# Pairing the heads in the features as they are paired in the work: new loads of a weight matrix, new sums, a new order

## The chip, the core and the metric

The kernel runs on one core of a Trainium2 chip. A core has TensorE (matrix products, written to PSUM), VectorE (DVE), ScalarE (ACT), GpSimd (POOL), SyncE (SP, which here only issues transfers), an on-chip memory (SBUF) of 128 partitions, and 16 DMA engines that carry the transfers between device memory and SBUF. The metric is the device time of one execution in microseconds, as the median of several runs.

## The reference

Causal attention over 4 batches, 8 heads, 768 positions of 64 features. Heads 0, 2 and 6 see everything up to their own position ("retrieval"); heads 1, 3, 4, 5 and 7 see the first 4 positions and a window of the last 64. Then a feed-forward layer over all 3072 tokens, with the 8 x 64 attention outputs as the 512 features:

```
scores = q @ k.T / sqrt(64)
a = softmax(where(mask[head], scores, -1e9))
x = (a @ v) laid out as (3072 tokens, 8 heads x 64)
h = x @ w_in                          # 512 x 2048
g = h * sigmoid(beta * h)
out = g @ w_out                       # 2048 x 512, float32
```

All inputs and the output are float32; the kernel computes its products in bfloat16.

## The kernel before

The work is cut into 8 units of 384 query positions, two for each batch: u = 0 is the first half of a sequence, u = 1 the second; a unit's number is n = 2b + u. For each unit the kernel transposes queries and keys, computes scores, exponentials and masks, sums and products with V (`attention`), normalizes them into `xT` (features in partitions, tokens in columns), and runs the feed-forward layer: 16 blocks of hidden features through `mm1`, tanh and multiply (`first`), and 48 matmuls of `mm2` into three output tiles (`second`).

The 512 features stand in `xT` as four tiles of 128 partitions, two heads each. `PAIRS` (line 17) says which two heads share a tile of queries and keys, `XT` (line 18) which two share a tile of features. In the kernel before these differ in the first two tiles: `PAIRS` has (0, 2), (1, 3), while `XT` has (1, 0), (2, 3). `mm1` multiplies tile t of `xT` with tile t of `w_in`, so the rows of `w_in` must stand in the order of `XT`.

`load_w_in(s)` (line 473), for s = 0 to 3, brings a quarter of `w_in`'s columns (512 rows of 2 KB, 1 MB) into a staging tile `wf` of 128 partitions x 4 row tiles: one transfer for tiles 1 to 3, and one of 64 partitions for each half of tile 0, because its two heads stand in swapped order. `load_w_out(s)` brings 1 MB of `w_out` in one transfer. `wf` has three buffers, which later loads of q, k and v use too. POOL casts each quarter in four pieces into `w_in_sb`; four blocks of `mm1` need one quarter.

For units 2 to 7, the softmax sums go this way: `sums_d` (line 748) has TensorE add up each head's row in a PSUM bank, with the heads placed by `QUARTERS` and `ROWS`; `sums_copy` brings them to SBUF (`sc`); `sums_turn` (line 781) moves the rows into `rec`, 12 partitions a head, with one small transfer for each entry of `TURNS` (line 31), which are (first row, step, slot, number of rows); VectorE takes reciprocals; `spread_rows` moves `rec` into four rows of `R`, and `spread_lanes` copies these over the partitions. `norm` multiplies. Units 0 and 1 have another path for this, on TensorE.

All transfers but four at the start are issued by SP, in one queue. The order of the whole program is written out: `_Plan.add` collects 1102 operations with the engines that may do them, a cost and what they need; `SEQUENCE` (line 37) lists them in an order found beforehand, and `CHOICE` (line 92) names the engine of each of the 97 operations that have a choice. `_Plan.run` goes through the list, works out start times from the costs, hands out buffers, and gives the operations out by start time. On each engine they keep the order of `SEQUENCE`. In unit 0 and in `sink_rows`, `fill` puts extra matmuls on TensorE where the plan leaves it a gap.

Each engine works its list in order; a transfer on SP waits for its buffer, and for the semaphore of an earlier transfer, before it is issued, and everything behind it in the queue waits too.

Of the kernel before, what the change touches and what calls it, by code (L numbers as in the profile page):

```python
# [16 lines left out]
PAIRS = [(0, 2), (1, 3), (4, 5), (6, 7)]  # L17
XT = [(1, 0), (2, 3), (4, 5), (6, 7)]
# [10 lines left out]
QUARTERS = [[[1, 0], [4, 5], [2, 3], [6, 7]], [[2], [6], [0], [5, 1, 4, 3, 7]]]  # L29
ROWS = [16, 1]  # L30
TURNS = [[(0, 32, 0, 4), (16, 32, 4, 4)], [(97, 1, 0, 2), (0, 32, 2, 4), (99, 1, 6, 2)]]
# [6 lines left out]
    0, 472, 8, 10, 480, 2, 12, 14, 77, 485, 484, 474, 477, 1, 479, 4, 6, 9, 475, 481, 25, 33, 11, 35, 3, 27,  # L38
    13, 34, 483, 36, 53, 26, 42, 37, 15, 28, 44, 54, 78, 5, 39, 40, 38, 7, 100, 45, 55, 469, 29, 30, 47, 56,
    79, 80, 101, 89, 90, 57, 43, 31, 32, 41, 85, 470, 48, 471, 102, 112, 103, 50, 59, 51, 91, 60, 92, 114, 86,  # L40
    108, 116, 58, 81, 82, 49, 104, 115, 113, 134, 117, 109, 16, 135, 17, 23, 137, 138, 61, 52, 46, 62, 118,
    139, 105, 87, 88, 119, 110, 83, 84, 106, 120, 24, 140, 122, 121, 136, 123, 18, 19, 20, 63, 107, 21, 22,
    73, 74, 64, 75, 141, 111, 65, 66, 71, 67, 125, 159, 160, 76, 68, 69, 70, 126, 486, 487, 490, 128, 129,
    131, 132, 142, 143, 488, 72, 526, 530, 489, 534, 538, 124, 127, 130, 133, 496, 497, 500, 527, 528, 531,
    532, 535, 536, 539, 542, 543, 540, 498, 544, 546, 547, 548, 499, 553, 554, 555, 506, 507, 557, 558, 559,
    561, 562, 563, 510, 161, 162, 184, 508, 509, 95, 96, 565, 566, 567, 569, 93, 97, 94, 98, 99, 516, 518,
    144, 145, 185, 576, 577, 146, 570, 517, 571, 155, 157, 578, 156, 158, 519, 147, 148, 149, 580, 581, 150,
    151, 520, 193, 167, 196, 511, 515, 512, 514, 501, 513, 153, 152, 154, 503, 584, 505, 585, 588, 582, 194,
    598, 502, 586, 476, 599, 600, 589, 590, 602, 606, 610, 614, 607, 608, 603, 604, 611, 612, 615, 616, 491,
    492, 618, 619, 620, 625, 629, 168, 626, 627, 504, 494, 633, 171, 630, 637, 641, 634, 631, 635, 638, 639,  # L50
    648, 652, 169, 493, 529, 642, 495, 643, 649, 650, 653, 654, 170, 188, 189, 533, 172, 592, 593, 173, 174,
    190, 191, 521, 656, 657, 163, 523, 164, 524, 594, 537, 165, 166, 186, 522, 525, 658, 187, 192, 541, 545,
    549, 550, 552, 219, 220, 221, 556, 560, 203, 206, 207, 564, 204, 660, 664, 665, 666, 661, 222, 568, 572,
    575, 223, 226, 198, 201, 199, 601, 605, 609, 482, 573, 662, 613, 617, 225, 621, 624, 628, 224, 205, 175,
    176, 200, 195, 197, 202, 208, 209, 178, 177, 179, 229, 228, 227, 236, 632, 237, 238, 240, 239, 230, 233,
    579, 583, 587, 241, 243, 232, 242, 180, 591, 636, 478, 250, 244, 640, 644, 647, 210, 211, 251, 252, 231,
    271, 273, 253, 645, 245, 248, 246, 247, 595, 551, 596, 574, 254, 651, 249, 181, 212, 255, 655, 256, 659,
    663, 182, 258, 183, 213, 215, 622, 217, 257, 275, 259, 260, 261, 214, 667, 216, 218, 670, 646, 668, 671,
    674, 678, 672, 272, 682, 686, 675, 676, 679, 680, 683, 318, 288, 684, 687, 688, 690, 276, 279, 691, 692,
    697, 698, 699, 701, 705, 702, 274, 703, 278, 709, 706, 707, 262, 263, 710, 713, 720, 711, 724, 281, 721,  # L60
    722, 277, 320, 280, 292, 234, 714, 715, 725, 726, 291, 293, 728, 729, 730, 732, 736, 322, 319, 323, 264,
    295, 737, 733, 623, 669, 673, 321, 235, 677, 297, 300, 324, 734, 298, 681, 685, 689, 738, 693, 694, 302,
    305, 303, 289, 301, 325, 696, 700, 265, 266, 267, 306, 282, 283, 285, 268, 269, 270, 704, 708, 712, 716,
    717, 299, 327, 296, 294, 304, 742, 746, 290, 750, 326, 743, 744, 747, 748, 328, 337, 335, 370, 751, 752,
    307, 718, 338, 754, 339, 284, 755, 758, 759, 308, 340, 342, 756, 341, 760, 286, 762, 769, 773, 777, 336,
    763, 764, 349, 374, 373, 377, 774, 775, 309, 778, 350, 779, 329, 770, 771, 310, 311, 372, 719, 723, 380,
    781, 782, 785, 727, 783, 371, 352, 375, 786, 787, 792, 695, 343, 287, 793, 794, 344, 345, 347, 348, 796,
    800, 801, 802, 378, 797, 798, 376, 379, 731, 354, 357, 346, 358, 312, 313, 804, 805, 808, 355, 356, 735,
    739, 740, 314, 316, 315, 317, 390, 745, 806, 749, 753, 809, 810, 353, 391, 392, 394, 417, 395, 351, 418,
    757, 814, 815, 761, 765, 766, 767, 816, 330, 818, 819, 822, 826, 830, 820, 823, 824, 827, 828, 396, 397,  # L70
    387, 831, 832, 359, 360, 768, 834, 841, 835, 842, 836, 421, 843, 332, 331, 772, 333, 399, 361, 334, 362,
    776, 780, 784, 788, 791, 845, 846, 401, 847, 849, 789, 795, 422, 404, 850, 405, 851, 597, 393, 853, 854,
    857, 398, 799, 420, 424, 855, 858, 859, 402, 864, 865, 868, 869, 803, 866, 872, 876, 403, 870, 400, 880,
    873, 874, 363, 381, 364, 365, 807, 811, 812, 790, 406, 368, 407, 881, 882, 419, 423, 366, 367, 817, 813,
    821, 877, 825, 829, 878, 833, 837, 838, 369, 886, 887, 890, 894, 382, 408, 409, 384, 888, 891, 892, 895,
    896, 840, 898, 899, 902, 906, 900, 903, 904, 383, 907, 908, 427, 425, 426, 436, 435, 437, 438, 913, 917,
    410, 411, 921, 922, 923, 918, 919, 844, 385, 848, 852, 386, 914, 915, 388, 389, 428, 431, 925, 926, 927,
    439, 441, 440, 856, 860, 412, 861, 863, 415, 413, 414, 929, 936, 416, 930, 937, 938, 931, 867, 871, 940,
    839, 941, 942, 434, 448, 451, 452, 875, 879, 883, 449, 884, 443, 444, 445, 958, 962, 446, 447, 963, 964,
    959, 960, 944, 948, 949, 450, 950, 453, 945, 946, 966, 970, 741, 974, 967, 968, 971, 972, 975, 976, 889,  # L80
    430, 885, 978, 952, 953, 954, 979, 893, 980, 897, 901, 905, 909, 912, 454, 456, 457, 455, 442, 985, 986,
    987, 458, 916, 459, 460, 910, 989, 990, 993, 997, 429, 432, 433, 991, 862, 998, 999, 461, 462, 920, 924,
    928, 932, 935, 939, 933, 1001, 1008, 994, 995, 1012, 1013, 1014, 1009, 943, 947, 951, 955, 1010, 1002,
    1003, 1016, 473, 1020, 1021, 956, 463, 464, 961, 465, 466, 467, 1024, 1025, 1022, 965, 969, 973, 934, 468,
    1030, 1017, 1018, 977, 1026, 981, 982, 984, 1031, 1032, 983, 1034, 1038, 1035, 1036, 988, 992, 1039, 1042,
    1040, 1043, 1046, 1044, 1047, 1048, 1050, 1051, 1052, 996, 1057, 1061, 1065, 1058, 1059, 911, 1062, 1063,
    1066, 1067, 1000, 1004, 1005, 1007, 1069, 1070, 1073, 1071, 1074, 1075, 1079, 1080, 1081, 957, 1011, 1082,
    1085, 1083, 1084, 1015, 1086, 1087, 1088, 1091, 1089, 1092, 1033, 1037, 1041, 1045, 1090, 1049, 1006,
    1093, 1053, 1056, 1054, 1060, 1064, 1068, 1072, 1076, 1055, 1077, 1019, 1023, 1027, 1028, 1078, 1094,
    1095, 1029, 1098, 1096, 1097, 1099, 1100, 1101,  # L90
]
CHOICE = (
    "dgddadggggdddaaddaadgggaadadgdggdgggddddaadadaadgadaddagdadgdddgagggdggaaaaaadaaaaadaaaadadadadda"
# [95 lines left out]
def kernel(  # L189
# [15 lines left out]
    B, H, S, D = q.shape  # L205
# [267 lines left out]
    def load_w_in(s):  # L473
        f = stg.tile([128, 2048], F32, name="wf", bufs=RINGS["wf"]).rearrange("p (a n) -> p a n", a=NP)

        def rows(r, n, tiles):
            return bass.AP(moe_w_in.tensor, moe_w_in.offset + r * d_ff + s * 2 * FS,
                           [[d_ff, n], [128 * d_ff, tiles], [1, 2 * FS]])
        sp.dma_start(out=f[:, 1:4, :], in_=rows(128, 128, 3))
        sp.dma_start(out=f[0:D, 0:1, :], in_=rows(D, D, 1))  # L480
        sp.dma_start(out=f[D:128, 0:1, :], in_=rows(0, D, 1))
        wst["i", s] = f
# [706 lines left out]
    for u in range(2):  # L1189
        add("dve", 0.75, lambda u=u: const_mask_new(u), gives=[("const", "new", u)],  # L1190
            needs=[("M", u, pi, ri) for pi in range(NP) for ri in range(len(rounds_of(pi, u))) if mask_cost(pi, ri, u)] + [("const", "mask", 0)])
        add("dve", [0.9, 0.7][u], lambda u=u: const_mask_s(u), needs=[("const", "m")], gives=[("const", "mask", u)])
# [56 lines left out]
```

## Time and profile before

| | |
|---|---|
| time, median of 3 runs | 246.41 us (244.87 to 246.75) |
| the profiled execution | 243.74 us, of which 242.0 from its first to its last instruction |
| busy: TensorE, VectorE, ScalarE, POOL | 221.8, 161.5, 138.9, 87.8 us |
| mean granted TensorE clock | 0.993 |
| read from device memory, written | 27.57 MB, 6.29 MB |
| `mm1`, 512 matmuls of 128x384 | 91.5 us busy |
| `mm2`, 375 matmuls of up to 128x512 that the trace holds | 87.4 us busy |

Busy times come from the records of one execution; products on TensorE are pipelined, so their busy time is a bound on the time that it has work. Each line of a chain or a timeline begins with its start and its duration in microseconds. Almost every instruction carries line 112 (a helper through which all are issued), so the names of the tiles tell them apart: `b<-xT,w_in` is `mm1`, `b<-w_out,gT` is `mm2`, `wf<-in_moe_w_in_dram` a load of `w_in`, `rec<-sc` the turn of the sums, `R<-rec` their spreading. A letter q behind an engine (SPq) means its queue of instructions that issue transfers or wait.

### The profile page before, as it was taken

Reading aid. Unit: us, or ns where it says so; the run is one execution under the profiler, and the core shown is the slowest. Engines: PE = TensorE matmul, PEld = TensorE weight load, DVE = VectorE, ACT = ScalarE, POOL = GpSimd, SP = SyncE. Lnnn points to the kernel's source line nnn. Section 1 sums busy time; section 2 is a strip of 40 time slices with the busy share of each in tenths; the row PEclk is TensorE's granted clock in tenths of the full one; section 3 lists DMA queues with packets and bytes.
Section 4 is the critical chain, followed back from the end, with each engine's and each line's share of the span. In section 5 each row is a group of like instructions: output and inputs, shape, how many; then the busy total and the mean of one; then the engine's idle time right before and its main releaser. Section 6 shows DMA issues by size and latency. Waiting matters only on the chain.

```text
span 242.0 us, 6040 instructions
## 1 busy us (share of the span) xinstructions
PE 221.8 (92%) x2327; PEld 125.8 (52%) x2352; DVE 161.5 (67%) x390; ACT 138.9 (57%) x232; POOL 87.8 (36%) x200
## 2 busy tenths in 40 slices
PE   7788888899999888797999899999999999999995
PEld 7545454465544454453555455555555555655544
DVE  5879957887383658777679458877777465655311
ACT  2878854784537647553895675517668543346300
POOL 6441673687605247313751725350390000000000
PEclk9979999999999999999999999999999999999999
DMA  6999999999999396889979971746901011031022
GB/s 203 309 235 286 252 216 315 352 325 214 202 191 221 72 255 121 154 222 170 253 156 179 152 168 48 173 118 74 217 3 43 3 47 47 3 130 44 2 87 88
DMA packets 90003, 38.41 MB, mean 159 GB/s; under 512 B 76518, under 2 KB 82934, under 8 KB 89974
## 3 DMA queue, kind: packets, MB, share of 16 engines
q1 hardware_dynamic: 88886, 37.24, 66.4%
q10 hardware_dynamic: 1088, 0.79, 1.0%
q8 instruction: 18, 0.29, 0.5%
q14 instruction: 11, 0.09, 0.1%
HBM read 27.57 MB, written 6.29 MB: 140 GB/s over the span
## 4 chain that ended last, share of the span: by engine, by line
PE 54%; DMA 21%; SPq 13%; POOL 4%; DVE 4%; issue 3%; ACT 1%; POOLq 0%; DVEq 0%
PE b L112 49%; SPq L112 13%; DMA wf<-in_moe_w_in_dram 10%; PE sp L112 4%; DMA QK<-c 4%; DMA wf<-in_k_dram 3%; DMA q2f<-in_q_dram 2%; POOL c L112 2%; DMA wf<-in_v_dram 2%; DVE es L112 1%; DVE QK L112 1%; POOL w_in L112 1%; DVE c L112 1%; DVE mask_s L112 1%; POOL vs L112 1%
## 5 line engine op out<-in xcount | busy, mean ns | idle before, releaser
L112 ACT ACTIVATE t<-b,beta_h 128x384 f32<-128x384 f32 x128 | 71.6, 581 | 45.9 <-PE b L112 37.6
L112 PE MATMUL b<-xT,w_in 128*128 128x384 bf16 x512 | 91.5, 326 | 3.5 <-POOL w_in L112 2.0
L112 DVE SCALAR_TENSOR_TENSOR gT<-t,b 128x384 bf16<-128x384 f32 x128 | 68.3, 550 | 33.5 <-ACT t L112 30.6
L112 PE MATMUL b<-w_out,gT 128*128 128x512 bf16 (+1 forms) x375 | 87.4, 370 | 2.1 <-issue 1.3
L112 PEld LDWEIGHTS <-w_in 128*128 128x128 bf16 x512 | 48.6, 98 | 40.7 <-POOL w_in L112 3.4
L112 ACT ACTIVATE es<-sp 128x768 bf16<-128x768 f32 (+3 forms) x64 | 48.8, 806 | 15.4 <-PE sp L112 15.1
L112 PEld LDWEIGHTS <-gT 128*128 128x128 bf16 x400 | 37.4, 98 | 38.3 <-issue 1.8
L112 POOL CAST c<-wf 128x256 bf16<-128x256 f32 x60 | 24.9, 463 | 22.9 <-DMA wf<-in_k_dram 18.6
L112 PE MATMUL sp<-QK 64*64 64x64 bf16 (+7 forms) x402 | 19.5, 237 | 6.7 <-DMA QK<-c 5.3
L112 ACT ACTIVATE osb<-b 128x512 f32<-128x512 f32 (+1 forms) x18 | 10.6, 589 | 25.9 <-PE b L112 25.9
L112 PEld LDWEIGHTS <-QK 64*64 64x64 bf16 (+1 forms) x402 | 10.2, 105 | 19.0 <-issue 14.8
L112 POOL CAST vb<-wf 128x512 bf16<-128x512 f32 x18 | 11.2, 644 | 24.3 <-DMA wf<-in_v_dram 19.0
L112 DVE TENSOR_TENSOR es<-es,mask_c 128x256 bf16<-128x256 bf16 (+2 forms) x32 | 9.9, 331 | 10.0 <-ACT es L112 10.0
L112 DVE TENSOR_TENSOR es<-es,mask_s 128x800 bf16<-128x800 bf16 (+5 forms) x24 | 13.9, 585 | 3.6 <-ACT es L112 3.6
L112 DVE TENSOR_TENSOR xT<-sp,R 128x768 bf16<-128x768 f32 (+3 forms) x21 | 12.7, 630 | 3.5 <-PE sp L112 3.3
L112 POOL CAST w_in<-wf 128x512 bf16<-128x512 f32 x16 | 9.2, 625 | 12.6 <-DMA wf<-in_moe_w_in_dram 12.6
L112 PE MATMUL sp<-es,vb 128*64 128x64 bf16 (+3 forms) x243 | 13.8, 237 | 0.0
L112 DVE TENSOR_SCALAR osb<-b 128x512 f32<-128x512 f32 (+1 forms) x7 | 4.6, 653 | 12.4 <-PE b L112 10.1
L112 DVE STREAM_SHUFFLE R<-R 128x768 f32<-128x768 f32 (+1 forms) x15 | 12.7, 873 | 0.1
L112 PEld LDWEIGHTS <-vb 128*64 128x64 bf16 x243 | 11.5, 111 | 0.5
L112 POOL COPY KP<-QK 128x64 bf16<-128x64 bf16 (+5 forms) x32 | 8.4, 305 | 9.1 <-DMA QK<-c 8.4
L112 POOL CAST w_out<-wf 128x512 bf16<-128x512 f32 x16 | 9.5, 639 | 2.9 <-DMA wf<-in_moe_w_out_dram 2.9
(90 smaller groups left out, 172.2 us busy)
## 6 DMA issues: line engine op xcount, KB each, us to landing
out_dram<-osb SPq DMA_DIRECT2D x23, 256.0 KB
wf<-in_v_dram SPq DMA_DIRECT2D x18, 256.0 KB
wf<-in_moe_w_out_dram SPq DMA_DIRECT2D x4, 1024.0 KB
wf<-in_q_dram SPq DMA_DIRECT2D x15, 256.0 KB
wf<-in_k_dram SPq DMA_DIRECT2D x15, 256.0 KB
wf<-in_moe_w_in_dram SPq DMA_DIRECT2D x4, 768.0 KB
q2f<-in_q_dram SPq DMA_DIRECT2D x12, 192.0 KB
k2f<-in_k_dram SPq DMA_DIRECT2D x8, 192.0 KB
```

The costliest lines, as they stand in the source:

```text
L112: ins = f(*a, **k)
```

## The change

`XT` becomes the same as `PAIRS`: the first two feature tiles hold heads (0, 2) and (1, 3). So tile t (0 or 1) of `w_in` takes its upper 64 rows from head t and its lower 64 from head t + 2. `load_w_in` still issues three transfers for a quarter: tiles 2 and 3 in one of 512 KB, and tile 0 and tile 1 in one of 256 KB each, from a source of 2 x 64 rows into 128 partitions.

The sums' placing follows: `QUARTERS` has other heads in each bank quarter, and `TURNS` has three transfers for u = 0 instead of two, and four for u = 1 instead of three. Costs in the plan change (those of the sums' transfers on SP, of the weight loads, of one mask), and with them the whole `SEQUENCE` and `CHOICE`: the order of operations is new on every engine. On SP, of the operations around the weights, the two first loads of unit 2 (q and k of pair 0) move from among the loads of `w_in` to behind the first two loads of `w_out`. On TensorE the first blocks of `mm1` stay in their order.

```diff
-XT = [(1, 0), (2, 3), (4, 5), (6, 7)]
+XT = PAIRS
...
-QUARTERS = [[[1, 0], [4, 5], [2, 3], [6, 7]], [[2], [6], [0], [5, 1, 4, 3, 7]]]
+QUARTERS = [[[0, 3], [4, 7], [1, 2], [6, 5]], [[0], [6], [2], [5, 4, 1, 3, 7]]]
 ROWS = [16, 1]
-TURNS = [[(0, 32, 0, 4), (16, 32, 4, 4)], [(97, 1, 0, 2), (0, 32, 2, 4), (99, 1, 6, 2)]]
+TURNS = [[(0, 32, 0, 4), (80, 32, 4, 2), (16, 32, 6, 2)], [(0, 1, 0, 1), (97, 1, 1, 2), (32, 32, 3, 3), (99, 1, 6, 2)]]
...
     def load_w_in(s):
...
-        def rows(r, n, tiles):
-            return bass.AP(moe_w_in.tensor, moe_w_in.offset + r * d_ff + s * 2 * FS,
-                           [[d_ff, n], [128 * d_ff, tiles], [1, 2 * FS]])
-        sp.dma_start(out=f[:, 1:4, :], in_=rows(128, 128, 3))
-        sp.dma_start(out=f[0:D, 0:1, :], in_=rows(D, D, 1))
-        sp.dma_start(out=f[D:128, 0:1, :], in_=rows(0, D, 1))
+        at = moe_w_in.offset + s * 2 * FS
+        cols = [1, 2 * FS]
+        sp.dma_start(out=f[:, 2:4, :], in_=bass.AP(moe_w_in.tensor, at + 4 * D * d_ff, [[d_ff, 128], [2 * D * d_ff, 2], cols]))
+        for t in range(2):
+            sp.dma_start(out=f[:, t, :], in_=bass.AP(moe_w_in.tensor, at + t * D * d_ff, [[2 * D * d_ff, 2], [d_ff, D], cols]))
...
-                add(e, 0.47, lambda pi=pi, nm=nm, e=e: load_qk(x, pi, nm, ENG[e]), dma=0.6,
+                add(e, 0.47, lambda pi=pi, nm=nm, e=e: load_qk(x, pi, nm, ENG[e]), dma=0.65,
...
-            add("sp", [0.8, 1.2][u], lambda: sums_turn(x), needs=[("sum_s", n)], gives=[("sum_t", n)], dma=0.2,
+            add("sp", [1.3, 2.1][u], lambda: sums_turn(x), needs=[("sum_s", n)], gives=[("sum_t", n)], dma=0.2,
...
-            add("sp", 1.7, lambda: spread_rows(x), needs=[("rec", n)], gives=[("rd", n)], dma=0.1,
+            add("sp", [2.6, 2.9][u], lambda: spread_rows(x), needs=[("rec", n)], gives=[("rd", n)], dma=0.1,
...
-        add("dve", 0.75, lambda u=u: const_mask_new(u), gives=[("const", "new", u)],
+        add("dve", 1.5, lambda u=u: const_mask_new(u), gives=[("const", "new", u)],
...
-            add("sp", 1.3 if w == "i" else 0.65, lambda s=s, ld=ld: ld(s), dma=3.2, gives=[("wf", w, s)], begun=[("begun", w, s)],
+            add("sp", 1.6 if w == "i" else 0.6, lambda s=s, ld=ld: ld(s), dma=3.1 if w == "i" else 2.9, gives=[("wf", w, s)], begun=[("begun", w, s)],
```

An access pattern is written as a list of [step, count], the outermost first. The new values of `SEQUENCE` and `CHOICE` are left out.

## The prediction

> **What bounds the kernel now.** I read four views of the profiled execution: the page's forty slices, the chain that ended last in order of time, the waits, and the windows by stage. Then I read the transfers of the first 60 us one by one: the issue of each, the updates of its semaphore, and its packets' durations, all of which the trace records.
>
> The slices first (one digit per 6.05 us: TensorE busy, granted clock, DMA engines busy, in tenths):
>
> ```profile
> PE   7788888899999888797999899999999999999995
> PEclk9979999999999999999999999999999999999999
> DMA  6999999999999396889979971746901011031022
> ```
>
> The DMA engines are full for the first 13 slices (79 us) and nearly idle in the last 11. TensorE is the reverse. So there are two regimes: up to some 134 us what arrives decides, afterwards TensorE's own work does. The chain says the same and names the transfer:
>
> ```profile
> 14.86 0.34 SPq L112
> 15.24 6.90 DMA wf<-in_moe_w_in_dram
> 22.16 9.00 DMA wf<-in_moe_w_in_dram
> 31.23 0.08 issue
> 31.31 0.63 POOL w_in L112
> ...
> 32.75 7.11 DMA wf<-in_moe_w_in_dram
> 39.93 0.08 issue
> 40.01 1.19 POOL w_in L112 x2
> 41.19 0.05 issue
> 41.24 0.99 PE b L112 x5
> ```
>
> From 15 to 40 us the chain is the loads of the first weight matrix, the very transfers that the change rewrites. They end in the POOL casts of the last quarter (s = 3), and at 41.24 us TensorE starts the first product that needs them, `mm1(0, 12)`. Whatever delays that landing delays TensorE: its order is fixed, and its remaining list is full:
>
> ```profile
> core 0: us, PE busy (x) PEld busy (x) DVE busy (x) ACT busy (x) POOL busy (x), PEclk, DMA share, GB/s
> 36.00:42.00 6.00, 4.88 (x82) 3.10 (x73) 5.01 (x11) 2.65 (x4) 1.99 (x4) 1.00 1.03 306
> 48.00:54.00 6.00, 6.00 (x37) 3.54 (x37) 4.82 (x11) 4.95 (x11) 4.85 (x11) 1.00 1.09 333
> 180.00:200.00 20.00, 19.79 (x170) 10.66 (x171) 12.38 (x25) 11.80 (x21) 1.21 (x1) 1.00 0.08 28
> ```
>
> POOL's wait for these loads, today 12.6 us in four pieces (total, times, longest), is the wait to watch:
>
> ```profile
> POOL w_in L112 <- DMA wf<-in_moe_w_in_dram: 12.6, 4, 5.2
> ```
>
> **How many engines carry a transfer.** The issue rows that matter (name, count, KB each):
>
> ```profile
> wf<-in_moe_w_in_dram SPq DMA_DIRECT2D x4, 768.0 KB
> wf<-in_moe_w_in_dram SPq DMA_DIRECT2D x8, 128.0 KB
> R<-rec SPq DMA_DIRECT2D x18, 6.0 KB
> rec<-sc SPq DMA_DIRECT2D x9, 6.0 KB
> rec<-sc SPq DMA_DIRECT2D x6, 3.0 KB
> ```
>
> All weight rows here show 16 updates of the semaphore per transfer, over 2 to 3.4 us. The 6 KB `rec<-sc`, whose source is 4 rows x 12 pieces, shows 5; the 3 KB ones (2 rows x 12 pieces into 24 partitions) show 3; the loads of 8 x 8 pieces 9; the 6.5 KB `R<-rec` of 52 partitions 14; the 6 KB one of 48 partitions 16. In each case this is one more than the largest number up to 16 that divides the outermost counts of both sides (2 and 24 give 2; 4 and 48 give 4; 52 gives 13), except that a full 16 has no extra update. I read it as: that many engines work, and one update fills up the rest.
>
> The new load of tile 0 or 1 has a source of [2 heads][64 rows][2 KB] and a destination of 128 partitions: outermost counts 2 and 128. By these rows it runs on two engines, just as the 2-row `rec<-sc` does. Before, its two halves had 64 and 64, hence 16. The transfer of tiles 2 and 3 keeps 128 outermost and its 16 engines.
>
> The Trainium skill, "DMA: Bandwidth & Descriptors", section "Why a DMA increments its semaphore by 16 and not by 1", states this as a rule: the split takes the slowest dimension that isn't 1 of each side and the largest divisor up to 16 of both, and on this kind of queue always the lowest-numbered engines. The counts above agree with it; no row here shows which two engines they are. By the page both tiles share one pair and the sum below stands; on two pairs the packets below would fall from 144 to 80 per quarter, and the delay from 28.6 to some 7 us.
>
> Against it stands "Trainium Kernel Development and Optimization", section "Best Practices": always tile to 128 partitions. That would make the change a gain. The rows give that little room: the eight 64-partition pieces landed 0.38 to 0.78 us after the one before, 0.57 on average, where 128 KB at the pace of the 768 KB pieces (2.65 and 2.86 us for quarters 1 and 2) takes 0.46. So 8 x 0.11 = 0.9 us, if the new transfers keep 16 engines.
>
> **The parts and their prices.** A 2 KB packet occupies its engine for 84 ns (median of 7,040; 82 at the 10th percentile; 102 median at 20 to 30 us, when all engines pull weights). Per quarter, 1 MB is 512 packets.
>
> - *Loads of w_in, on the path.* Before: 32 packets on each engine, 2.7 us at 84 ns; landings were in fact 3.85 and 3.88 us apart (23.43, 27.28, 31.16 us). After: the two loaded engines get 16 + 64 + 64 = 144 packets, 12.1 us. The queue order is also new: the first of unit 2's query loads now stands behind the weights, so they start at the third value load's landing, 17.2 us, not at 17.8. Then 29.3, 41.4 and 53.5 us; the three value loads between (2.85 us before, from 31.56 to 34.41) 56.4; the last quarter 68.5, against 39.86. That is **+28.6 us**. It hides behind nothing. TensorE's order up to `mm1(0, 12)` holds the same work as before (only a transpose of unit 2 moves out and one normalization product in), so it stands idle some 10 us ahead of each quarter. Every later load passes the same two engines, so all are late alike. Bounds: 82 ns gives +27.5; 120 ns (3.86 us over 32 packets, the pace while 16 engines pulled) gives +49. I take 84, the row for a lone stream: output stores at 75 to 80 us, with few others running, show it too.
> - *Clock.* A TensorE that idles shows a lower granted clock: 0.79 at 12 to 18 us and 0.93 at 18 to 24. That is 1.26 to 1.7 us of lost clock; after the last wait it lies on the path. Bounds 0 and 1.7, taken **+1.3**.
> - *Unit 2's loads.* Between the last quarter's landing and unit 2's last key load lie 15.0 us now (four w_out, six q/k loads); in the new order eight q/k loads, two more by 0.6 us: **+1.2**, as TensorE meets the transposes of unit 2 next. Bounds 0 and 2.5.
> - *The turn of the sums.* Two transfers become three for even units, three become four for odd ones, from unit 2 on: six more issues at 0.66 us (median of the `rec<-sc` issues), 3.9 us of SP's queue. Behind them on SP stand output stores and blocks of later units; VectorE's reciprocals wait for them. The chain runs along SP's queue from 71 to 134 us, where three of the six units turn: 2.0 us exposed; the rest lies beside TensorE's full list. Bounds 0 and 3.9, taken **+1.3**.
> - *Head order in the sums and products with V.* The matmuls are the same in number and size; the two column halves have one full and one windowed head each, as now. Zero; were a tenth of the 28.8 us that the products with V are busy (13.8, 9.6 and 5.4 in the groups from vb, vs and VE) to lose its overlap, 2.9 us.
> - *The new order and engine choices.* 4 operations fewer on VectorE, 5 more on ScalarE, one fewer on POOL. Neither bounds a stage. TensorE's idle time from 42 to 230 us adds up to about 10 us in the windows, so the order can give back at most that; it can lose as much. Taken 0, bounds -5 and +5.
>
> Sum: 28.6 + 1.3 + 1.2 + 1.3 = 32.4 us. The profiled execution took 243.74 us (span 242.0), so 276.1 on its own scale; the median of the runs, 246.41, lies 2.7 above it: 278.8. The idle SP queue and VectorE during the long wait may let some small work run ahead; I take off 2 and say **277 us**.
>
> **Rivals.**
> 1. *The new transfers use 16 engines after all* (the program hands the dimensions over in another order): not slower. The 0.9 us gained and 1.3 lost on the turns cancel, and the new order decides: 246 us, 241 to 251. Against it: the 3 updates of the 2-row `rec<-sc`. It decides from 8 engines up: there the loaded engines have 16 + 16 + 16 = 48 packets a quarter, 4.0 us, about today's 3.85.
> 2. *A slower or uneven pair*: rows at 8 KB pitch may keep the 120 ns pace: 246.4 + 49 + 4 = 299 us. For it: weight packets reached 140 ns at the upper quartile at 20 to 30 us; against: that was with 16 engines at it.
> 3. *Two pairs of engines*, one per tile: 246.4 + 7 + 4 = 257 us. For it: no row shows the pair. Against: none shows a rotation either.
>
> **Chances.** Forecast 0.74, rival 1 0.09, rival 2 0.09, rival 3 0.08. About 1% is what runs of this kernel can tell from no change (they spread over 0.8%). Rival 1 alone holds times near or below today's: faster 0.04, same 0.03, slower 0.93. The forecast's own range, 270 to 287, comes from its bounds; for 8 in 10 it reaches partly into rivals 2 and 3: 261 to 294.
>
> **What would show it.** The page's issue rows should have eight w_in transfers of 256 KB, each with 3 updates of its semaphore, 5 us apart or more. DMA busy should fall to one or two tenths between 20 and 65 us, POOL's wait for w_in should grow from 12.6 to some 40 us, and `mm1(0, 12)` should start near 69 us. From there to the end the trace should look like the present one from 41 us on, about 200 us. I am wrong if these transfers show 16 updates, or if the weights land late and the time between `mm1(0, 12)` and the end shrinks by more than 5 us.

## The result, and the profile after

The changed kernel takes 279.36 us (median of 4 runs, 278.78 to 280.40) against 245.64 us for the kernel before in the same runs: 1.1388 times as long, with a 95% interval of 1.1299 to 1.1477. The profiled execution took 279.21 us, 277.5 of them from the first instruction to the last. The medians here and below take in all executions of a kernel, single ones of which ran far longer than the rest (up to 779 us), while the ratios go by the fast executions alone.

The slices of the changed kernel, one digit per 6.94 us (TensorE busy, its granted clock, DMA engines busy, in tenths):

```profile
PE   8794413086499999985899998999999999999995
PEclk9997575559689999999799999999999999999999
DMA  7953222278589998594889779968700112000203
```

Where the kernel before has its DMA engines full, the new one has a valley: the digits 3, 2, 2, 2, 2 from 21 to 56 us. TensorE starves beside it, and its clock falls to a half. After some 73 us both rows look much like those of before from 41 us on.

The issue rows show the transfers as the diff has them (name, count, KB each):

```profile
wf<-in_moe_w_in_dram SPq DMA_DIRECT2D x4, 512.0 KB
wf<-in_moe_w_in_dram SPq DMA_DIRECT2D x8, 256.0 KB
```

The DMA view of the changed kernel between 24 and 36 us, again in 40 slices, now of 0.3 us (busy share in tenths, then GB/s), shows what carries them:

```profile
DMA  1111111111111111111111111111111138997954
GB/s 48 55 48 48 55 48 48 48 48 55 48 48 55 48 48 55 41 55 55 41 55 48 41 41 48 55 48 48 55 48 48 61 96 239 300 253 232 335 184 130
```

For 9.6 us the row reads 1: two engines of 16 are 0.125. They move 41 to 61 GB/s in a slice, most often 48, and 48.8 GB/s is two packets of 2 KB every 84 ns. The packets' times say it directly: from 25 to 33 us there are never fewer than two packets under way, and exactly two in 90% of that time. Then come 96 to 335 GB/s, as the 512 KB transfer of quarter 2 uses the other engines too. Each of the eight new transfers has 3 updates of its semaphore in the trace, and each of the 512 KB ones 16. The last updates of the weight loads and of the three value loads between them, in us:

```
quarter 0:  512 KB 19.13   tile 0 24.65   tile 1 29.93
quarter 1:  512 KB 31.50   tile 0 37.23   tile 1 42.50
quarter 2:  512 KB 44.05   tile 0 49.37   tile 1 54.83
values:     55.70  56.74  57.63
quarter 3:  512 KB 59.90   tile 0 65.65   tile 1 72.54
```

Tile follows tile on the same two engines, 5.3 to 5.7 us each in the first three quarters (64 packets of 84 ns are 5.4). The last updates of a 512 KB transfer come after tile 1 of the quarter before, 1.6 us later in quarters 1 and 2: its share on the loaded pair waits there.

The chain that ended last, with start and duration of each piece (the 5.38 us of "issue" from 37.23 to 42.61 hold the landing of quarter 1's tile 1 at 42.50):

```profile
20.81 16.41 DMA wf<-in_moe_w_in_dram
37.23 5.38 issue
42.61 1.74 POOL w_in L112 x3
...
56.07 16.47 DMA wf<-in_moe_w_in_dram
72.69 0.62 POOL w_in L112
73.36 9.53 PE b L112 x45
```

In the kernel before, the same last step, from POOL's cast into `mm1(0, 12)`, came at 41.24 us. TensorE's idle stretches lie ahead of each quarter, as the windows show (window, length, then busy us and count of TensorE, its weight loads, VectorE, ScalarE, POOL, then clock, DMA share, GB/s):

```profile
24.00:30.00 6.00, 0.51 (x4) 0.11 (x3) 0.96 (x4) 1.33 (x3) 0.00 (x0) 0.51 0.13 49
36.00:42.00 6.00, 0.00 (x0) 0.00 (x0) 0.89 (x3) 0.20 (x1) 0.00 (x0) 0.65 0.14 53
48.00:54.00 6.00, 0.00 (x0) 0.00 (x0) 0.34 (x1) 0.00 (x0) 0.00 (x0) 0.50 0.30 86
72.00:78.00 6.00, 4.64 (x15) 2.03 (x16) 2.17 (x5) 1.16 (x2) 4.71 (x9) 0.50 0.38 104
```

And the waits (total us, times, longest) name the cause and who passes it on:

```profile
POOL w_in L112 <- DMA wf<-in_moe_w_in_dram: 36.1, 3, 13.6
PEld L112 <- POOL w_in L112: 33.1, 5, 9.8
PE b L112 <- POOL w_in L112: 30.6, 4, 9.1
```

### The profile page after: what moved, and what is told of

Its sections match the earlier page's. It is cut to its first block, busy times and chain, and to the rows that moved or that the text cites. A ratio compares the mean times of both kernels' runs of the same rounds, so it can differ in the third digit from the quotient of the medians.

```text
span 277.5 us, 6060 instructions
## 1 busy us (share of the span) xinstructions
PE 230.8 (83%) x2334; PEld 128.3 (46%) x2359; DVE 163.4 (59%) x386; ACT 140.4 (51%) x237; POOL 88.6 (32%) x199
## 4 chain that ended last, share of the span: by engine, by line
PE 53%; DMA 20%; SPq 11%; issue 5%; DVE 4%; ACT 3%; POOL 3%; ACTq 0%; DVEq 0%; POOLq 0%
PE b L112 47%; DMA wf<-in_moe_w_in_dram 12%; SPq L112 11%; PE sp L112 5%; DMA QK<-c 2%; DMA q2f<-in_q_dram 2%; ACT es L112 2%; DMA R<-rec 2%; DMA out_dram<-osb 2%; ACT t L112 2%; POOL c L112 1%; DVE es L112 1%; DVE gT L112 1%; DVE QK L112 1%; POOL w_in L112 1%
## 5 line engine op out<-in xcount | busy, mean ns | idle before, releaser
L112 PE MATMUL b<-xT,w_in 128*128 128x384 bf16 x512 | 99.2, 347 | 31.4 <-POOL w_in L112 30.6
L112 ACT ACTIVATE t<-b,beta_h 128x384 f32<-128x384 f32 x128 | 72.5, 583 | 77.4 <-PE b L112 66.3
L112 PE MATMUL b<-w_out,gT 128*128 128x512 bf16 (+1 forms) x375 | 86.4, 373 | 2.2 <-issue 1.4
L112 PEld LDWEIGHTS <-w_in 128*128 128x128 bf16 x512 | 51.1, 103 | 74.5 <-POOL w_in L112 33.1
L112 POOL CAST c<-wf 128x256 bf16<-128x256 f32 x60 | 23.0, 425 | 27.5 <-DMA wf<-in_k_dram 17.1
L112 PE MATMUL sp<-QK 64*64 64x64 bf16 (+6 forms) x402 | 18.7, 235 | 5.7 <-DMA QK<-c 4.5
L112 DVE TENSOR_TENSOR es<-es,mask_s 128x800 bf16<-128x800 bf16 (+5 forms) x24 | 15.3, 646 | 0.8 <-ACT es L112 0.6
L112 DVE TENSOR_TENSOR es<-es,mask_c 128x256 bf16<-128x256 bf16 (+2 forms) x32 | 12.9, 415 | 2.5 <-ACT es L112 2.1
L112 POOL COPY KP<-QK 128x360 bf16<-128x360 bf16 (+3 forms) x30 | 8.9, 343 | 15.6 <-DMA QK<-c 13.1
L112 DVE TENSOR_TENSOR xT<-sp,R 128x768 bf16<-128x768 f32 (+3 forms) x21 | 12.6, 628 | 2.0 <-PE sp L112 1.8
L112 POOL COPY vs<-vb 64x1536 bf16<-64x1536 bf16 (+2 forms) x9 | 11.9, 1330 | 0.4
```

The lines of the kernel that those rows point to most:

```text
L112: ins = f(*a, **k)
```

## The experiments

Each timed kernel stood beside runs of the kernel before on the same chip (medians 244.3 to 244.8 us); the ratios go by these. A half is one of the two transfers of 64 partitions that bring tiles 0 and 1 in experiment 1.

| | kernel | median us | ratio to before (95%) |
|---|---|---|---|
| 1 | changed, weights by halves on 16 engines | 248.93 | 1.016 (1.009 to 1.023) |
| 9, 12 | the same again | 248.62, 248.04 | 1.018 (1.012 to 1.024), 1.016 (1.012 to 1.020) |
| 2 | changed, only tile 0 in the new form | 262.31 | 1.069 (1.062 to 1.077) |
| 3 | changed layout and loads, old order | 281.55 | 1.150 (1.142 to 1.157) |
| 4 | as 3, weights by halves | 250.67 | 1.024 (1.014 to 1.034) |
| 5, 10 | as 1, two turns in even units | 247.63, 247.51 | 1.012 (1.009 to 1.016), 1.012 (1.008 to 1.016) |
| 6 | as 1, a turn for every row | 261.63 | 1.069 (1.064 to 1.074) |
| 7 | changed, TensorE kept busy before the last quarter | 281.19 | 1.150 (1.146 to 1.154) |
| 8 | before, with the added turns | 245.83 | 1.005 (1.001 to 1.009) |
| 11 | before's layout and loads, new order | 244.82 | 1.001 (0.997 to 1.005) |

**1. The same rows, other outermost count.**

```diff
-        for t in range(2):
-            sp.dma_start(out=f[:, t, :], in_=bass.AP(moe_w_in.tensor, at + t * D * d_ff, [[2 * D * d_ff, 2], [d_ff, D], cols]))
+        for i in range(2):
+            sp.dma_start(out=f[i * D:(i + 1) * D, 0:2, :],
+                         in_=bass.AP(moe_w_in.tensor, at + i * 2 * D * d_ff, [[d_ff, D], [D * d_ff, 2], cols]))
```

> The changed kernel, but tiles 0 and 1 of w_in arrive as two transfers of 64 partitions x 2 tiles (heads 0 and 1 into the upper half, 2 and 3 into the lower), 64 rows outermost on both sides; still three transfers a quarter, all else and the order as changed. Theory (two engines carry each new tile transfer, and that alone delays everything): these show 16 updates of the semaphore, quarters land some 4 us apart, mm1(0, 12) starts near 41 us, and the time is 242 to 250 us. Rival (the new order or the added turns of the sums cost the time): 272 us or more, with the first weights early.

248.93 us, and 16 updates for every transfer. Same bytes, same number of transfers, same order; the outermost count went from 2 to 64, and each transfer fills half of the partitions of both tiles instead of all partitions of one. Some 30 us of the 34 are gone. The DMA row of the page and the chain of this kernel:

```profile
DMA  6999999999997495989987997792001120100313
```

```profile
14.11 6.89 DMA wf<-in_moe_w_in_dram
21.02 10.82 DMA wf<-in_moe_w_in_dram
31.98 2.48 POOL w_in L112 x4
```

The valley has closed and the three first quarters are in at 31.84 us (54.83 in the changed kernel). `mm1(0, 12)` starts at 41.3 us. The theory holds for the bulk; some 4 us over the kernel before are left, which the later runs take up.

**2. Half the dose.**

```diff
-        for t in range(2):
-            sp.dma_start(out=f[:, t, :], in_=bass.AP(moe_w_in.tensor, at + t * D * d_ff, [[2 * D * d_ff, 2], [d_ff, D], cols]))
+        sp.dma_start(out=f[:, 0, :], in_=bass.AP(moe_w_in.tensor, at, [[2 * D * d_ff, 2], [d_ff, D], cols]))
+        for i in range(2):
+            sp.dma_start(out=f[i * D:(i + 1) * D, 1, :], in_=bass.AP(moe_w_in.tensor, at + (1 + 2 * i) * D * d_ff, [[d_ff, D], cols]))
```

> The changed kernel, but tile 1 of w_in arrives as two transfers of 64 partitions; tile 0 keeps the new form, four transfers a quarter. Theory: the two loaded engines carry 16 + 64 + 8 = 88 packets of 84 ns a quarter, 7.4 us instead of 12.1, so from 17.2 us the quarters land at 24.6, 32, 39.4 and, behind the value loads, 49.7 us: 20 us or more earlier than in the changed kernel, for 255 to 262 us. Rival (tiles 0 and 1 use different pairs of engines, or the price is a latency for each transfer): within 5 us of 279 or of 246.

262.31 us, just past the upper end. Quarters 0 to 2 were complete at 26.73, 34.41 and 41.88 us: 7.7 and 7.5 apart where 88 packets of 84 ns are 7.4. In the changed kernel they are 12.3 to 12.6 us apart, where one shared pair has 144 packets (12.1 us) and two pairs would have 80 each (6.7). So both tiles of the changed kernel share one pair, and the rival of two pairs falls. A fixed price for each such transfer would have halved here too, as half of them are left; against it stands the trace of the changed kernel, in which two packets are under way all the time that such a transfer takes.

**3 and 4. The old order.** The kernel before with the new `XT`, `QUARTERS`, `TURNS` and `load_w_in` (as the change has them, or as in experiment 1); `SEQUENCE`, `CHOICE` and costs stay as before.

> The kernel before with the new XT, QUARTERS, TURNS and load of w_in, but its old costs, order and choice of engines. Theory: the loads cost the same whatever the order, so 275 to 286 us. Rival (the new order is what costs): 245 to 255 us.

> The same with the two transfers of 64 partitions x 2 tiles of the first experiment: new head pairs, new turns, 16 engines, old order. Theory: 245 to 250 us, from the kernel before's 246 plus up to 4 us for six more turn transfers in an order that wasn't found for them. The difference from the first experiment is what the new order is worth; I take it as 0 to 4 us in its favour.

281.55 and 250.67 us, the second just past its upper end: the loads cost some 31 us in the old order as they do 30 in the new one. What is left with 16 engines, 1.4 to 3.4% (its two lowest executions took 247.60 and 249.37 us), is there in the old order too, so it does not take the new order to bring it. In whose favour the new order is, the two intervals (1.4 to 3.4% here, 0.9 to 2.3% in experiment 1) do not tell.

**5 and 10. Three turns fewer.**

```diff
-QUARTERS = [[[0, 3], [4, 7], [1, 2], [6, 5]], [[0], [6], [2], [5, 4, 1, 3, 7]]]
+QUARTERS = [[[0, 2], [4, 5], [1, 3], [6, 7]], [[0], [6], [2], [5, 4, 1, 3, 7]]]
-TURNS = [[(0, 32, 0, 4), (80, 32, 4, 2), (16, 32, 6, 2)], [(0, 1, 0, 1), (97, 1, 1, 2), (32, 32, 3, 3), (99, 1, 6, 2)]]
+TURNS = [[(0, 32, 0, 4), (16, 32, 4, 4)], [(0, 1, 0, 1), (97, 1, 1, 2), (32, 32, 3, 3), (99, 1, 6, 2)]]
```

> The first experiment's kernel (16 engines for the weights, new order), but QUARTERS for even units pairs the heads so that the sums turn in two transfers, as in the kernel before, instead of three: three issues of 0.66 us fewer on SP in units 2, 4 and 6. Theory (the turns cost about 0.2 us each of the end, 1.3 for six): 0.5 to 1 us below the first experiment, within its noise. Rival (the turns are the whole of its 4 us over the kernel before): 2 us or more below it.

> The kernel with 16 engines and two turns in even units, once more, on the same chip. If three turns fewer are worth 0.5 us each, 1.5 us below the one beside it; and, with the new layout, the nearest to the kernel before that I have: 0.5 to 1.5% above it. If it comes out below the kernel before, the new pairs would be worth having with other loads.

1.3 and 1.1 us below the run of experiment 1's kernel in the medians; the second pair shares a chip. By the ratios 0.3 and 0.7%, and the intervals overlap. It has the sign and size of 0.4 us for each turn, no more can be said, and this kernel too stays above the kernel before.

**6. A turn for every row.**

```diff
-TURNS = [[(0, 32, 0, 4), (80, 32, 4, 2), (16, 32, 6, 2)], [(0, 1, 0, 1), (97, 1, 1, 2), (32, 32, 3, 3), (99, 1, 6, 2)]]
+TURNS = [[(p + i * st, 1, c + i, 1) for p, st, c, n in t for i in range(n)]
+         for t in [[(0, 32, 0, 4), (80, 32, 4, 2), (16, 32, 6, 2)], [(0, 1, 0, 1), (97, 1, 1, 2), (32, 32, 3, 3), (99, 1, 6, 2)]]]
```

> The first experiment's kernel with every row of the sums turned by a transfer of its own: eight a unit instead of three (even) or four (odd), 27 more issues on SP over six units, 17.8 us of its queue at 0.66 us each. It doubles and more the suspected cost. Theory (SP's queue hides two thirds): 5 to 8 us above the first experiment. If the turns are hidden: within 2 us of it. If all of it is exposed: 15 us or more above.

261.63 us, 13 us over experiment 1's kernel for 27 more issues: 0.48 us each, above the 5 to 8 us of the case hidden by two thirds and below the 15 of the exposed one. VectorE's reciprocals, which wait for the turned sums, show it: the idle time ahead of them is 16.6 us in all, against 2.4 in experiment 1. The issues also took longer than I had reckoned: 48 held SP's queue for 35.2 us, 0.73 each on average.

**7. A warm clock.**

```diff
         h = bank(("h", x.n, fi))
+        for _ in range(90 if (x.n, fi) == (0, 12) else 0):
+            pe.matmul(h[:, 0:128], w_in_sb[0][:, 0, 0:128], x.xT[:, 0, 0:128], start=True, stop=True)
```

> The changed kernel with 90 more matmuls of 128 columns, results unused, just ahead of mm1(0, 12), where TensorE waits for the last weights: they run while it waits anyway. Theory (after the wait the granted clock is 0.50 for several us, which costs 2.5 us by the window from 72 to 84): the clock at mm1(0, 12) is 1.0 and the time falls by 1.5 to 3 us, to 276.5 to 278. Rival (other engines set the pace there, POOL's casts or the tanh): no change, 279 to 280.

281.19 us, above what either case expected; its interval and the changed kernel's overlap. The added matmuls ended at 70.8 us, 2.6 us too early, and the clock fell to 0.5 once more, but for 3.4 us instead of 6.8:

```profile
72.00:78.00 6.00, 4.60 (x20) 2.18 (x21) 2.31 (x5) 1.64 (x3) 4.67 (x9) 0.72 0.37 113
```

(the clock is the third number from the end; the changed kernel has 0.50 there). `mm2` starts 0.9 us earlier, at 87.5 us, and the lead grows: of the 512 `mm1` matmuls the 193rd starts at 145.5 us against 147.9. In the changed kernel the clock falls to 0.5 a second time, from 133.4 to 136.8 us, and here it doesn't. But the lead is lost again: from 168 to 172 us the chain of both kernels runs through a transfer `QK<-c`, TensorE waits for it for 2.0 us here and 0.8 in the changed kernel, and goes on at 172.2 us against 171.8. So there a transfer in SP's queue sets the time, and what TensorE gained before it doesn't reach the end. A clock that stays high throughout wasn't tried.

**8. The added turns alone.**

```diff
-TURNS = [[(0, 32, 0, 4), (16, 32, 4, 4)], [(97, 1, 0, 2), (0, 32, 2, 4), (99, 1, 6, 2)]]
+TURNS = [[(0, 32, 0, 4), (16, 32, 4, 2), (80, 32, 6, 2)], [(97, 1, 0, 2), (0, 32, 2, 2), (64, 32, 4, 2), (99, 1, 6, 2)]]
```

> The kernel before, with one of its turn transfers cut in two in every unit from 2 on: three for even units, four for odd ones, as in the changed kernel; nothing else. It asks what of the 4 us that remain with 16 engines is the turns'. Theory (the turns' price by the slope of the kernel with a transfer for every row, some 13 us for 27: 0.5 each): 2 to 4 us above the kernel before. Rival (the rest is the new order, or the new way of loading): within 1 us of it.

1.0048 (1.0011 to 1.0085) times the kernel before: 1.2 us (0.3 to 2.1). That is below the 2 to 4 us that the slope of experiment 6 made me expect.

**9. Experiment 1's kernel again.**

> The first experiment's kernel once more, on the same chip as the two beside it, to make the small differences comparable. 1.0 to 2.2% above the kernel before, as then.

1.018: 4.5 us over the kernel before.

**11 and 12. The new order alone.** The changed kernel's `SEQUENCE`, `CHOICE` and costs on the old `XT`, `QUARTERS`, `TURNS` and `load_w_in`; beside it experiment 1's kernel, on the same chip.

> The new order, choice of engines and costs alone, on the old layout: the kernel before's XT, QUARTERS, TURNS and load of w_in. It asks whether the 3 us that 16 engines and the turns leave unexplained are the new order's. If they are: 2 to 4 us above the kernel before. If they belong to the new pairs of heads (sums, products with V): within 1 us of it.

> Once more the first experiment's kernel, on the same chip as the one beside it: the new order with the new pairs, new turns and 16 engines, 1.2 to 2.4% above the kernel before. The difference of the two is what pairs, turns and halves cost together in the new order.

1.001 (0.997 to 1.005): on the old layout the new order costs and gains nothing that these runs can tell (-0.6 to 1.3 us). With pairs, turns and halves in the same order it is 1.016: 1.46% of 244.55 us more, 3.6 us (2.2 to 5.0 by the two intervals).

## Why the prediction was right

The forecast was 277 us, the time is 279.36; it was the forecast's mechanism, not one of the rivals. That the number came so close is partly luck, as the last step below shows. By its steps:

*Two engines.* Right, and it rests on four things: 3 updates on each transfer, a DMA busy share of one tenth at 48 GB/s, two packets under way at a time, and experiments 1 and 2, where the other outermost count brings back some 30 of the 34 us, and 17 when one of the two tiles has it. The rule of the Trainium skill ("DMA: Bandwidth & Descriptors", section "Why a DMA increments its semaphore by 16 and not by 1"), that a transfer runs on the largest number up to 16 that divides both slowest counts and on this queue always on the lowest-numbered engines, agrees with the 3 updates and with tiles that follow one another 5.3 us apart rather than side by side. Which engines they are the trace doesn't tell. The maxim "always tile to 128 partitions" ("Trainium Kernel Development and Optimization", section "Best Practices") does not decide here. The page says it of tensors in SBUF and PSUM, and the staging tile has 128 partitions in all these kernels; what differs is the transfers that fill it: 128 partitions at a time on two engines give 1.139 times the time of the kernel before, 64 at a time on 16 engines 1.016.

*The delay of the last quarter.* 28.6 us forecast; its landing moved by 32.7 (39.86 to 72.54) and `mm1(0, 12)` by 32.1 (41.24 to 73.36). The three first quarters took 12.3 to 12.6 us each, near 12.1. The last took 14.9, from 57.63 to 72.54, which is 2.8 of the 4 us. Two loads of `w_out`, behind it in the queue, ran at the same time. The DMA view from 60 to 72 us (slices of 0.3 us) shows them beside the pair, up to 64 us and again from 67:

```profile
DMA  4991699999999952119429479999999999999952
GB/s 89 205 89 61 232 362 389 382 328 321 280 266 273 259 137 68 48 41 96 157 68 123 82 259 423 362 355 253 321 307 321 253 279 251 256 259 255 241 124 50
```

The 2 KB packets of all engines took 127 ns at the median from 63 to 65 us and 125 from 69 to 71, the pace that I had put into the upper bound. The pair's own pace follows from the landings: tile 0 took 5.75 us and tile 1 6.89, which is 90 and 108 ns for each of 64 packets. The step that failed is "I take 84, the row for a lone stream": the last quarter isn't a lone stream.

*From there to the end.* The forecast has 1.3 for the clock, 1.2 for unit 2's loads and 1.3 for the turns, 3.8 together; the trace has 204.1 us from `mm1(0, 12)` to the end, against 200.8: 3.4. But the parts look wrong. Experiment 1's kernel, which has early weights and no idle TensorE there, takes 203.6 and 204.1 in its two traces (experiments 1 and 9), so clock and unit 2's loads add 0 to 0.5 us, not 2.5. Each of these figures is one execution, and executions of one kernel differ by 1 to 2 us, so this is an indication and no more. The two delays themselves are there: the clock fell to 0.5 for 6.8 us, and from the last quarter's landing to unit 2's last key load it is 15.8 us against 15.0, 0.8 of the 1.2 forecast. Experiment 7 shows a gain on TensorE lost at the wait for `QK<-c` at 172 us, so a delay ahead of it need not reach the end either. By these traces, what I had priced at 1.3 for turns and nothing for the new pairs is nearly all of it.

*The turns and the pairs.* Experiment 8 gives 1.2 us for the six turns in the old order: the term's size. On top of that the new layout costs about 2 us that I had put at zero: 3.6 between experiments 11 and 12, less 1.2, with an interval of 1 to 4 us. Part of it may be the turns once more, if they weigh more in this order. VectorE waits for the turned sums (idle before, in the kernel before, the new order alone, and experiment 1's kernel):

```profile
L112 DVE RECIPROCAL rec<-rec 96x32 f32<-96x32 f32 x6 | 2.0, 341 | 0.1
```

```profile
L112 DVE RECIPROCAL rec<-rec 96x32 f32<-96x32 f32 x6 | 2.1, 345 | 0.7 <-DMA rec<-sc 0.7
```

```profile
L112 DVE RECIPROCAL rec<-rec 96x32 f32<-96x32 f32 x6 | 2.1, 346 | 2.4 <-DMA rec<-sc 2.4
```

From 0.7 to 2.4 us in the same order (2.9 in the second trace of experiment 1's kernel). It isn't only their number: with three turns fewer, experiment 5 still has 2.2. The halves have no visible share: `mm1(0, 12)` starts at 41.3 and 41.9 us in the two traces of experiment 1's kernel and at 42.2 in that of experiment 11, and the difference lies behind it, 203.6 and 204.1 us to the end against 200.7. What remains, the turns' weight in this order or the placing of heads in the sums and the products with V, is open: no run separates them.

*The new order.* Forecast 0, with bounds of 5 us each way; experiment 11 has 0.1% (-0.3 to 0.5) on the old layout. Right.

*The 2 us taken off* for small work that could run ahead have no counterpart. Without them the sum was 278.8. Profiled execution against profiled execution the change cost 35.5 us where I had added up 32.4: 3.5 us too little up to `mm1(0, 12)` and some 2 on the new pairs, against 2 to 2.5 too much on clock and loads. The median hides this: I added 2.7 us to get from the profiled execution to the median of the kernel before, and the changed kernel's profiled execution lay at its median (279.21 and 279.36). So errors of several us cancelled, and the 277 owes some of its closeness to luck.

## What to carry to other kernels

Look at the outermost count of both sides of a transfer before its partitions or its size: a source written as [2][64 rows] ran on two engines, and the same rows written as [64][2], for half of the partitions at a time, ran on 16. Here the trace of the kernel before showed it ahead of the change, in the number of semaphore updates of a small transfer with such a shape (3 for a source of 2 rows). And price a slow transfer by everything queued behind it on its engines: here 2 MB of the weights ran on two engines, and the later loads, which use all 16, were complete only when their share on these two was.

## What the runs showed of the hardware

- One pair of engines moved some 48 GB/s, 84 ns at the median for each 2 KB packet on each engine, with 14 engines idle beside them. With loads of `w_out` beside them for part of the time, 64 packets of each engine of the pair took 5.75 and 6.89 us, 90 and 108 ns each; the 2 KB packets of all engines took 125 to 127 ns at the median while both ran.
- In experiment 7 TensorE's clock fell to 0.5 at 72.95 us, 2.15 us after the last of 90 matmuls that ran for 5.2 us without a break; in the changed kernel at 71.94 us, 4.8 us after the last matmul. It rose again 3.4 and 6.8 us later.
- The issue of one small transfer of the sums held SP's queue for 0.65 us on average in the kernel before (2 or 4 source rows), 0.66 in the changed one, and 0.73 in experiment 6 (one row). The same transfers as in the changed kernel took 0.72 in experiment 4, so the number of rows is not shown to be the reason.
